# Attention and a mixture of experts on one core: ScalarE issues the weight loads of experts 1 to 7, each two eighths of a product after the split that frees its place

## The chip, the cores and the metric

The kernel runs on one core of a Trainium2 chip. The metric is the time of one execution in microseconds (us) of device time; the median of several runs stands for a kernel. A core has five engines that each take their instructions in order: TensorE (PE, matrix products; its weight loads are shown as PEld), VectorE (DVE), ScalarE (ACT), GpSimd (POOL) and SyncE (SP), which here only issues transfers. Sixteen DMA engines move the data. SP and ACT each feed a DMA queue of their own (q1 and q10 in the profile); POOL feeds a third (q0) with gathers and scatters.

## What is computed

Attention over 8 batches of 8 heads, 576 positions and 64 values a head, with scores below the row's maximum minus tau masked away, and then a mixture of experts on the 4608 rows of 512 values that it gives: each row goes to the one expert with the largest gate logit.

```python
scores = scale * np.matmul(q, k.transpose(0, 1, 3, 2))
thresh = np.max(scores, axis=-1, keepdims=True) - tau
scores = np.where(scores >= thresh, scores, -1000000000.0)
attn = exp(scores - max);  attn = attn / (sum + 1e-09)
x = matmul(attn, v), laid out as (4608, 512)
logits = x @ w_gate;  expert_idx = np.argmax(logits, axis=1)
for e in range(8):
    xe = x[expert_idx == e]
    out[expert_idx == e] = gate_w * (np.maximum(xe @ w1[e], 0.0) @ w2[e])
```

## The kernel before

**The order of the work.** The program is written as a walk over steps `k`. A step computes one tile of scores twice (L294 to L306 for the maxima, L342 to L368 for the transposed scores, the exponential and the mask) and one piece of the product with the values (L400 to L409). Everything else is put into lists by step (`plan`, `after`, `chain`) or by eighths of a product (`moe(c, ready, f)`: run `f` at the c-th eighth, or later when `ready()` holds). An eighth is 12 products of 128 columns on TensorE; the counter is `chunk[0]`. After the program is written, a scheduler moves instructions inside each engine's list by a simulated time of its own, so the built order isn't the written one.

**Rows to experts.** When a batch is finished, `finish(b)` makes the rows `x`: POOL or DVE normalise (L454), ACT casts the high part (L461), DVE or POOL the low part (L462), SP issues one DMA transpose per 128 rows into `xTg` (L469), and TensorE computes the logits (L483). `route` and `ranks` then run on DVE: the logits are reduced (L489), the winner is marked (L509 to L516), `run` counts (L520), TensorE ranks the rows (L528 to L531, `rk`), and DVE makes the place of each row, `posi` (L534 to L541), and ACT the gate (L524, L542). POOL scatters each tile of 128 rows to a DRAM array `xs` sorted by expert (L549). Batch 7, the last, has five tiles.

**The experts.** Each expert has four slots of 128 rows (slots 0 to 31; slots 0 to 7 go one by one, the others in pairs), and four late slots of 192 rows take what is left over. `fetch(m)` gathers the rows of a slot (L744, POOL), transposes them (L747, SP) and copies the gate (L750, DVE) and the destination (L755, POOL). The two tiles named `spare` hold slots 3 and 4. `gemm1` (L792) and `gemm2` (L819) are the two products; ACT takes the ReLU (L780) and the result (L830), POOL scatters it to the output (L831). The first fetches of a batch-7 row need the scatters before them, so on POOL scatters to `xs` and gathers of slots 5, 6 and 7 alternate.

**The weights.** An expert's weights come in eight pieces of 128x1024 f32 (512 KB), named `wf_e_c_w` (expert e, piece c of 4, w = 0 for the first product's matrix and 1 for the second's). `load_w` issues the load; `split_w` makes two f16 parts of it, the high part on ACT (L710), then the low part on DVE (L711). Expert 0 has two places for its pieces, all others share eight. `wseq` lists the pieces in the order of their splits. The first eight of experts 1 and up are loaded by `close`, when the attention's buffers are given back; from then on the split of piece j is followed at once by the load of piece j + 8, on SP, whose list also holds the transposes of L469 and L747.

Of the kernel before, what the change touches and what calls it, by code (L numbers as in the profile page):

```python
# [50 lines left out]
def kernel(  # L51
# [9 lines left out]
    nc = tc.nc  # L61
# [630 lines left out]
    def load_w(e, w, c):  # L692

        i = int(e != 0)
        wq[e, w, c] = wf = pools[i].tile([P, F], F32, tag="wf", name=f"wf_{e}_{c}_{w}", bufs=2 + 6 * i)
        if e in range(E):
            nc.sync.dma_start(wf, w12[e, :, c, w])
            return
        if e not in regs:
            regs[e] = nc.sync.value_load(T["esi"][0:1, e - E:e - E + 1], min_val=0, max_val=E - 1)  # L700
        nc.sync.dma_start(wf, w12[ds(regs[e], 1), :, c, w].rearrange("o p f -> (o p) f"))
# [3 lines left out]
    def split_w(e, w, c):  # L705
        wf = wq.pop((e, w, c))

        o = (wb1, wb2)[w][0 if e == "x" else e % 2][:, c].rearrange("p (a h d) -> p a h d", a=w + 1, h=2)
        x = wf.rearrange("p (a d) -> p a d", a=w + 1)
        nc.scalar.activation(o[:, :, 0], x, AF.Copy, scale=SW)  # L710
        nc.vector.scalar_tensor_tensor(o[:, :, 1], x, SW, o[:, :, 0], ALU.mult, ALU.subtract)  # L711
# [229 lines left out]
    def room():  # L941
        ldp.close()
        open_pool(0)
        load_w(*wseq[0])
        load_w(*wseq[1])

    def close():
        apool.close()
        open_pool(1)
        for i, x in enumerate(wseq[8:16]):  # L950
            after(W1D * i, lambda x=x: load_w(*x))

    wseq = [(0, w, c) for w in range(2) for c in range(4)]
# [11 lines left out]
    chunk = [0]  # L965
    wait = []

    def moe(c, ready, f):
        mo.setdefault(c, []).append((ready, f))
# [49 lines left out]
    def weights(j):  # L1019
        turn[0] = j + 1  # L1020
        split_done.add(wseq[j])
        split_w(*wseq[j])
        if j + 8 < len(wseq):
            load_w(*wseq[j + 8])

    for j, (k, *x) in enumerate(when):
        moe(k, lambda x=x: may(*x), lambda j=j: weights(j + 8))
# [123 lines left out]
```

## Time and profile before

| | us |
|---|---|
| median of 3 runs | 1066.05 (1059.29 to 1070.53) |
| the profiled execution | 1071.58 |
| its span, which the trace covers | 1069.9 |

The trace is of one execution on the only core, some 1.7 us shorter than the device's time of that execution. TensorE is the busiest engine. The span falls into the attention (up to some 600 us), a passage in which the last batches are routed while the first experts begin (some 600 to 740 us), the experts at full speed (740 to 992 us) and the late slots (992 us to the end).

### The profile page before, as it was taken

To read this page: it belongs to the slowest core of one execution; us is meant where nothing else is said; L and a number is where in the kernel's file an instruction comes from. 1 tells how busy PE (TensorE), PEld (TensorE's weight loads), DVE (VectorE), ACT (ScalarE), POOL (GpSimd) and SP (SyncE) were. 2 spreads that over 40 slices of the span, in tenths; PEclk is the share of its full clock that TensorE was granted. 3 is DMA by queue.
4 is the path that set the end of the run, shared out by engine and by line. 5 is a ranking of instruction groups with operands and counts; after the bars stand their busy time and mean duration, and the time that the engine had idled before them with its cause. 6 is when DMAs were issued, how large, how long until landed. Compare 5 with 4: busy or idle time off the path is not lost.

```text
span 1069.9 us, 27336 instructions
## 1 busy us (share of the span) xinstructions
PE 955.9 (89%) x10856; PEld 618.6 (58%) x10856; DVE 722.1 (67%) x1443; ACT 650.7 (61%) x1066; POOL 558.6 (52%) x460
## 2 busy tenths in 40 slices
PE   3799999898999999998995697877999999999995
PEld 1355555465565565564653484656677667667683
DVE  6899989788888889997889854732533423424650
ACT  2588887886888878988776653512433433424641
POOL 3266876976887958969768654143122121222121
PEclk9999999999999999999997799898999999999998
DMA  6534454664565635745535449759746656556720
GB/s 185 142 86 122 128 131 106 153 122 111 132 155 142 154 79 156 155 126 135 125 97 149 90 133 244 221 188 242 220 119 199 184 145 216 148 158 212 224 89 24
DMA packets 142558, 159.10 MB, mean 149 GB/s; under 512 B 96345, under 2 KB 112731, under 8 KB 142428
## 3 DMA queue, kind: packets, MB, share of 16 engines
q1 hardware_dynamic: 126796, 100.35, 38.2%
q10 hardware_dynamic: 6480, 27.53, 8.7%
q0 software_dynamic: 9152, 29.45, 8.6%
q8 instruction: 86, 1.41, 0.6%
q14 instruction: 44, 0.36, 0.1%
HBM read 90.24 MB, written 19.44 MB: 103 GB/s over the span
## 4 chain that ended last, share of the span: by engine, by line
PE 50%; DMA 17%; DVE 11%; issue 9%; ACT 6%; POOL 5%; SPq 2%; POOLq 0%; DVEq 0%; ACTq 0%
PE h L792 14%; PE y L819 12%; PE s L294 4%; PE st L342 4%; DVE e L362 3%; PE st L343 3%; PE s L296 3%; ACT e L359 3%; PE av L408 3%; PE av L409 3%; DMA CQ<-ptT 3%; DVE nm L306 3%; PE av L407 2%; DMA out_dram<-o,gt 2%; DMA xs<-R,posi 2%
## 5 line engine op out<-in xcount | busy, mean ns | idle before, releaser
L368 POOL TENSOR_TENSOR pl<-e,ph 128x1024 f16<-128x1024 f32 x158 | 337.1, 2145 | 135.0 <-ACT ph L367 105.5
L359 ACT ACTIVATE e<-st,ntau 128x512 f32<-128x512 f32 (+1 forms) x352 | 221.8, 651 | 45.6 <-PE st L343 39.4
L362 DVE SCALAR_TENSOR_TENSOR e<-st,e 128x512 f32<-128x512 f32 (+1 forms) x352 | 220.6, 638 | 29.9 <-ACT e L359 29.0
L306 DVE TENSOR_REDUCE nm<-s 128x1 f32<-128x512 f32 x320 | 200.3, 633 | 30.4 <-PE s L296 29.0
L792 PEld LDWEIGHTS <-wb 128*128 128x128 f16 x2304 | 193.2, 100 | 33.2 <-DMA xTm<-R 12.0
L792 PE MATMUL h<-xTm,wb 128*128 128x256 f16 (+2 forms) x2112 | 198.7, 256 | 12.9 <-DMA xTm<-R 12.5
L819 PE MATMUL y<-wb,hl 128*128 128x512 f16 (+1 forms) x1056 | 201.3, 360 | 0.3 <-issue 0.3
L367 ACT CAST ph<-e 128x1024 f16<-128x1024 f32 x160 | 166.4, 1041 | 11.2 <-DVE e L362 11.0
L408 PE MATMUL av<-vop,pl 128*128 128x65 f16 (+1 forms) x1280 | 161.1, 196 | 2.3 <-POOL pl L368 2.2
L294 PE MATMUL s<-QK 128*128 128x512 f16 (+3 forms) x640 | 139.2, 294 | 26.7 <-DMA QK<-lo 17.9
L407 PE MATMUL av<-vop,ph 128*128 128x64 f16 (+1 forms) x1280 | 162.6, 195 | 0.0
L409 PE MATMUL av<-vop,ph 128*128 128x65 f16 (+1 forms) x1280 | 161.8, 196 | 0.0
L342 PE MATMUL st<-QK 128*128 128x512 f16 (+3 forms) x640 | 139.1, 293 | 24.8 <-DVE e L362 15.8
L711 DVE SCALAR_TENSOR_TENSOR wb<-wf,wb 128x1024 f16<-128x1024 f32 x96 | 120.0, 1283 | 53.5 <-ACT wb L710 51.6
L819 PEld LDWEIGHTS <-hl 128*128 128x128 f16 (+1 forms) x1056 | 94.3, 100 | 98.9 <-issue 2.4
L343 PE MATMUL st<-CQ,ck 128*128 128x512 f16 (+3 forms) x640 | 137.7, 291 | 10.4 <-DMA CQ<-ptT 10.4
L408 PEld LDWEIGHTS <-pl 128*128 128x128 f16 (+1 forms) x1280 | 121.9, 101 | 28.3 <-POOL pl L368 9.0
L296 PE MATMUL s<-ck,CQ 128*128 128x512 f16 (+3 forms) x640 | 137.2, 290 | 0.0
L409 PEld LDWEIGHTS <-ph 128*128 128x128 f16 (+1 forms) x1280 | 121.8, 101 | 22.6 <-issue 10.6
L407 PEld LDWEIGHTS <-ph 128*128 128x128 f16 (+1 forms) x1280 | 122.4, 101 | 15.9 <-issue 6.5
L710 ACT ACTIVATE wb<-wf 128x1024 f16<-128x1024 f32 x96 | 97.5, 1050 | 41.9 <-DMA wf<-in_w_dram 21.8
L780 ACT ACTIVATE hl<-h 128x512 f16<-128x512 f32 (+1 forms) x80 | 45.6, 572 | 125.8 <-PE h L792 111.6
(189 smaller groups left out, 1147.0 us busy)
## 6 DMA issues: line engine op xcount, KB each, us to landing
wf<-in_w_dram SPq DMA_DIRECT2D x96, 512.0 KB
qkf<-in_qk_dram ACTq DMA_DIRECT2D x30, 576.0 KB
vf<-in_v_dram ACTq DMA_DIRECT2D x15, 640.0 KB
QK<-hi SPq DMA_DIRECT2D x64, 144.0 KB
QK<-hi SPq DMA_DIRECT2D x64, 72.0 KB
QK<-lo SPq DMA_DIRECT2D x64, 72.0 KB
ck<-lo SPq DMA_DIRECT2D x64, 72.0 KB
CQ<-hi SPq DMA_DIRECT2D x64, 64.0 KB
```

The source lines that it names most:

```text
L294: nc.tensor.matmul(sc[rows, oc], d["QA"][a][:, cols], d["KB"][a][:, CH[c]], start=True, stop=False)
L306: nc.vector.tensor_reduce(o, sc[:, 0:width(t)], axis=AX.X, op=ALU.max, negate=True)
L342: nc.tensor.matmul(sc[rows, oc], d["KB"][a][:, cols], d["QA"][a][:, CH[c]], start=True, stop=False)
L343: nc.tensor.matmul(sc[rows, oc], d["CK"][a][:, cols], d["CQ"][:, q], start=False, stop=True)
L359: nc.scalar.activation(pf, sc, AF.Exp, bias=ntau, scale=0.125 / SS)
L362: nc.vector.scalar_tensor_tensor(pf, sc, 0.0, pf, ALU.is_ge, ALU.mult)
L368: (nc.vector if (n, t) in PLV else nc.gpsimd).tensor_tensor(l, pd, h, ALU.subtract)
L407: nc.tensor.matmul(av[rows, a, 0:D], h, vop[:, tv, W:W + D], start=False, stop=False)
L408: nc.tensor.matmul(av[rows, a], l, vop[:, tv, 0:W], start=False, stop=False)
L409: nc.tensor.matmul(av[rows, a], h, vop[:, tv, 0:W], start=False, stop=a == 1 and i >= 2 and j == NT - 1)
L792: nc.tensor.matmul(o, Wt[:, c, wh, f], x, start=c == 0 and z == 0, stop=c == 3 and z == 2,)
L819: nc.tensor.matmul(o, h[:, hh], Wt[:, f, wh, c], start=f == 0 and z == 0, stop=f == 7 and z == 2)
```

## The change

The loads of experts 1 to 7 are issued by ACT in place of SP; those of expert 0 and of the late slots (whose expert is read from a register on SP) stay on SP. And each load after the first eight is put two eighths of a product behind the split, for the late slots too, while before it followed the split at once.

```diff
@@ load_w
         if e in range(E):
-            nc.sync.dma_start(wf, w12[e, :, c, w])
+
+            (nc.scalar if e else nc.sync).dma_start(wf, w12[e, :, c, w])
             return
@@ weights
         split_w(*wseq[j])
         if j + 8 < len(wseq):
-            load_w(*wseq[j + 8])
+
+            moe(chunk[0] + 2, lambda: True, lambda: load_w(*wseq[j + 8]))
```

The blank lines shift the lines of the changed kernel: L697 of before is L698, L710 is L711, L711 is L712, L747 is L748, L780 is L781. In the rows below, a name is tile, then its numbers (`wf_1_2_1` is expert 1, piece 2, second matrix), then the built program's own number. The scheduler also moves instructions that the change doesn't name.

SP in the passage, before: from the last of the first eight loads to the transposes of slots 3 and 4.

```order
L697 DMA wf_2_0_1_12851<-in_w12_dram 128x1024
L697 DMA wf_2_2_0_12885<-in_w12_dram 128x1024
L469 DMA_TRANSPOSE xTg_7_0_12717<-R_197 128x8x128 x2
L697 DMA wf_1_0_1_12890<-in_w12_dram 128x1024
L697 DMA wf_2_1_1_12950<-in_w12_dram 128x1024
L469 DMA_TRANSPOSE xTg_7_2_12736<-R_197 128x8x128 x2
L697 DMA wf_1_1_1_12966<-in_w12_dram 128x1024
L697 DMA wf_2_3_0_12971<-in_w12_dram 128x1024
L469 DMA_TRANSPOSE xTg_7_4_12747<-R_197 128x8x128
L697 DMA wf_1_2_1_13057<-in_w12_dram 128x1024
L747 DMA_TRANSPOSE spare_12675<-spare_12675 128x8x128 x2
```

The same place now:

```order
L469 DMA_TRANSPOSE xTg_7_0_12717<-R_197 128x8x128 x2
L469 DMA_TRANSPOSE xTg_7_2_12736<-R_197 128x8x128 x2
L469 DMA_TRANSPOSE xTg_7_4_12747<-R_197 128x8x128
L748 DMA_TRANSPOSE spare_12675<-spare_12675 128x8x128 x2
L748 DMA_TRANSPOSE xTm_5_13130<-R_197 128x8x128
```

The loads have left SP's list, and the transposes follow one another.

ACT in the passage, before: the casts of batch 7 (L461) and the splits of expert 1's first matrix.

```order
L710 ACTIVATE wb1_1_12629<-wf_1_0_0_12659 128x1024
L710 ACTIVATE wb1_1_12629<-wf_1_1_0_12724 128x1024
L461 CAST R_197<-xn_7_2_12713 128x4x128
L710 ACTIVATE wb1_1_12629<-wf_1_2_0_12755 128x1024
L461 CAST R_197<-xn_7_3_12722 128x4x128
L830 ACTIVATE o_0_0_12761<-y_0_0_12702,gt_0_0_11605 128x512
L461 CAST R_197<-xn_7_4_12732 128x4x128
L710 ACTIVATE wb1_1_12629<-wf_1_3_0_12835 128x1024
```

The same place now:

```order
L711 ACTIVATE wb1_1_12629<-wf_1_0_0_12659 128x1024
L698 DMA wf_2_0_1_12875<-in_w12_dram 128x1024
L698 DMA wf_1_0_1_12888<-in_w12_dram 128x1024
L711 ACTIVATE wb1_1_12629<-wf_1_1_0_12724 128x1024
L711 ACTIVATE wb1_1_12629<-wf_1_2_0_12755 128x1024
L461 CAST R_197<-xn_7_2_12713 128x4x128
L461 CAST R_197<-xn_7_3_12722 128x4x128
L698 DMA wf_2_2_0_12934<-in_w12_dram 128x1024
L698 DMA wf_2_1_1_12960<-in_w12_dram 128x1024
L711 ACTIVATE wb1_1_12629<-wf_1_3_0_12833 128x1024
L698 DMA wf_1_1_1_12966<-in_w12_dram 128x1024
L461 CAST R_197<-xn_7_4_12732 128x4x128
```

The loads stand between splits and casts; the first of all, `wf_1_0_0`, stands right behind L420, the last copy out of the attention's product. Further on, the load `wf_1_2_1` stands behind the split of `wf_1_0_1`, and `wf_1_3_1` behind that of `wf_1_2_1`.

DVE where batch 7 is routed, before:

```order
L516 TENSOR_REDUCE lg_7_12895<-oh_7_12942 128x8
L711 SCALAR_TENSOR_TENSOR wb2_1_12630<-wf_1_2_1_13057,wb2_1_12630 128x2x512
L520 TENSOR_TENSOR run_151<-run_151,lg_7_12895 128x8
L534 TENSOR_TENSOR rk_7_13019<-rk_7_13019,base_e_116 128x40
L536 TENSOR_REDUCE rk_7_13019<-ex_7_12943 128x5
L537 TENSOR_TENSOR rk_7_13019<-rk_7_13019,oh_7_12942 128x40
L538 TENSOR_SCALAR sm_7_12944<-rk_7_13019 128x5
L539 TENSOR_REDUCE rk_7_13019<-rk_7_13019 128x5
L540 RECIPROCAL sm_7_12944<-sm_7_12944 128x5
L711 SCALAR_TENSOR_TENSOR wb2_1_12630<-wf_1_3_1_13127,wb2_1_12630 128x2x512
L541 CAST posi_7_12946<-rk_7_13019 128x5
```

The same place now:

```order
L516 TENSOR_REDUCE lg_7_12893<-oh_7_12942 128x8
L520 TENSOR_TENSOR run_151<-run_151,lg_7_12893 128x8
L712 SCALAR_TENSOR_TENSOR wb2_1_12630<-wf_1_2_1_13057,wb2_1_12630 128x2x512
L534 TENSOR_TENSOR rk_7_13019<-rk_7_13019,base_e_116 128x40
L536 TENSOR_REDUCE rk_7_13019<-ex_7_12943 128x5
L537 TENSOR_TENSOR rk_7_13019<-rk_7_13019,oh_7_12942 128x40
L538 TENSOR_SCALAR sm_7_12944<-rk_7_13019 128x5
L539 TENSOR_REDUCE rk_7_13019<-rk_7_13019 128x5
L540 RECIPROCAL sm_7_12944<-sm_7_12944 128x5
L541 CAST posi_7_12946<-rk_7_13019 128x5
L712 SCALAR_TENSOR_TENSOR wb2_1_12630<-wf_1_3_1_13127,wb2_1_12630 128x2x512
```

The split of `wf_1_2_1` has moved behind `run`, that of `wf_1_3_1` behind `posi`. A little further on, DVE's copy `gt_5` (L750), which waits for a gather, now stands ahead of the splits of expert 2 and of the low parts of slot 3's and 4's ReLU, where before it stood behind most of them.

TensorE at the ranks of batch 7, before, where they stand behind the first 36 products of slot 3:

```order
L792 MATMUL h_3_0_12980<-spare_12675,wb1_0_11086 128x128
L528 LDWEIGHTS before_103
L528 MATMUL rk_7_13019<-oh_7_12942,before_103 128x8
L531 LDWEIGHTS ones_101
L531 MATMUL rk_7_13019<-was_7_12945,ones_101 128x8
```

The same place now, where they follow the logits:

```order
L483 MATMUL lg_7_12893<-wg_137,xTg_7_4_12747 128x16
L528 LDWEIGHTS before_103
L528 MATMUL rk_7_13019<-oh_7_12942,before_103 128x8
L531 LDWEIGHTS ones_101
L531 MATMUL rk_7_13019<-was_7_12945,ones_101 128x8
```

All of slot 3's first product now stands behind the ranks. Eight products of slot 6's `gemm2` that stood ahead of slot 7's `gemm1` now stand behind it.

## Rows read from the trace of the kernel before

**Rows 1.** The page's first line.

```profile
span 1069.9 us, 27336 instructions
```

**Rows 2.** Windows: length; PE, PEld, DVE, ACT, POOL busy; clock; DMA share; GB/s.

```profile
635.00:662.00 27.00, 26.69 (x289) 17.65 (x286) 16.50 (x32) 12.66 (x22) 11.49 (x8) 1.00 1.03 256
662.00:673.00 11.00, 1.02 (x25) 0.87 (x26) 3.11 (x11) 2.70 (x4) 1.67 (x3) 0.62 1.11 253
...
740.00:992.00 252.00, 252.00 (x1792) 173.83 (x1791) 93.98 (x124) 95.03 (x125) 53.42 (x71) 1.00 0.61 182
```

**Rows 3.** Waits of TensorE, 635 to 745 us: total, times, longest.

```profile
PE h L792 <- DMA xTm<-R: 12.5, 3, 7.8
PE lg L483 <- DMA xTg<-R: 8.4, 2, 5.1
```

**Rows 4.** Timeline of SP: start, duration, what it issued.

```profile
635.52 4.98 SPq L697 DMA_DIRECT2D wf<-in_w_dram  x8
...
651.57 6.24 SPq L469 DMA_TRANSPOSE xTg<-R  x2
657.90 1.01 SPq L697 DMA_DIRECT2D wf<-in_w_dram  x2
659.00 5.90 SPq L469 DMA_TRANSPOSE xTg<-R  x1
665.00 1.49 SPq L697 DMA_DIRECT2D wf<-in_w_dram  x1
```

**Rows 5.** Timeline of ACT; in brackets the idle time before and its releaser.

```profile
638.58 0.26 ACT L420 COPY xh<-av 64x130 f32<-64x130 f32 x1
...
655.02 1.06 ACT L710 ACTIVATE wb<-wf 128x1024 f16<-128x1024 f32 x1 [2.53 <-DMA wf<-in_w_dram]
...
668.00 1.06 ACT L710 ACTIVATE wb<-wf 128x1024 f16<-128x1024 f32 x1 [11.11 <-DMA wf<-in_w_dram]
...
671.93 1.06 ACT L710 ACTIVATE wb<-wf 128x1024 f16<-128x1024 f32 x1 [2.30 <-DMA wf<-in_w_dram]
...
678.34 1.06 ACT L710 ACTIVATE wb<-wf 128x1024 f16<-128x1024 f32 x1 [5.22 <-DMA wf<-in_w_dram]
```

**Rows 6.** Timeline of DVE where batch 7 is routed.

```profile
669.09 1.23 DVE L711 SCALAR_TENSOR_TENSOR wb<-wf,wb 128x1024 f16<-128x1024 f32 x1 [6.48 <-ACT wb L710]
...
671.09 0.25 DVE L489 TENSOR_REDUCE lg<-lg 128x40 f32<-128x80 f32 x1 [0.71 <-PE lg L483]
...
674.16 0.15 DVE L520 TENSOR_TENSOR run<-run,lg 128x8 f16<-128x8 f16 x1
677.50 0.21 DVE L534 TENSOR_TENSOR rk<-rk,base_e 128x40 f32<-128x40 f32 x1 [3.17 <-PE rk L531]
...
678.60 0.18 DVE L540 RECIPROCAL sm<-sm 128x5 f32<-128x5 f32 x1
679.43 1.23 DVE L711 SCALAR_TENSOR_TENSOR wb<-wf,wb 128x1024 f16<-128x1024 f32 x1 [0.65 <-ACT wb L710]
680.57 0.16 DVE L541 CAST posi<-rk 128x5 int32<-128x5 f32 x1
```

**Rows 7.** Timeline of TensorE.

```profile
672.95 4.00 PE L792 MATMUL h<-spare,wb 128*128 128x128 f16 x36 [1.90 <-DMA spare<-spare]
676.74 0.21 PE L528 MATMUL rk<-oh,before 128*128 128x8 f16 x1
...
727.49 7.93 PE L792 MATMUL h<-xTm,wb 128*128 128x128 f16 x92 [7.81 <-DMA xTm<-R]
...
736.53 3.61 PE L819 MATMUL y<-wb,hl 128*128 128x512 f16 x16 [0.34 <-issue]
```

**Rows 8.** Timeline of POOL: the first scatter of batch 7.

```profile
681.51 0.97 POOL L549 DMA_INDIRECT xs<-R,posi  x1 [10.30 <-DVE hl L781]
```

**Rows 9.** ACT's issues of L193 (loads of q and k): ns min/median/max.

```profile
L193 ACTq DMA_DIRECT2D qkf<-in_qk_dram x30: 334/335/412, 12.2 to 509.7; - x30
```

**Rows 10.** Waits in SP's list, whole span, longest total of weight loads.

```profile
SPq L697 <- DVE wb L711: 47.5, 27, 9.3
```

## The prediction

> **What bounds the kernel now.** I read the stages first, then the waits of TensorE, then each engine's timeline in the stretch where TensorE waits. The execution took 1071.58 us, 1.7 us more than its span [rows 1], and lies 5.5 us above the median of the three runs; the sum is made against the execution, and its difference is then applied to the median, 1066.05 us.
>
> From 740 to 992 us TensorE is busy for all of 252 us at the full clock [rows 2]. Most of the moved loads lie there, and nothing there can be gained. What can change is the passage before it. From 662 to 673 us TensorE works 1.02 of 11 us while the DMA share is 1.11: it waits for batch 7's transposes, and the DMA engines are full; they were already from 635 us on (1.03) [rows 2]. Later it waits 12.5 us in three pieces for the transposes of slots 5, 6 and 7, the longest 7.8 us [rows 3], which ends when slot 7 starts at 727.49 us [rows 7]. Slot 7's rows hang on the chain of scatters and gathers on POOL that begins at 681.51 us [rows 8]. POOL's row names a ReLU as its releaser; that is merely the last thing that DVE did. What the scatter needs is `posi`, done just before at 680.57 us [rows 6].
>
> So the question is when `posi` comes. In DVE's list the reduction of the logits (671.09 us) stands behind the low split of `wf_1_1_1` (669.09 us), and `posi` behind that of `wf_1_3_1` (679.43 us) [rows 6]. These splits follow ACT's at 668.00 and 678.34 us, which had waited 11.11 and 5.22 us for their loads [rows 5]. Of the loads, SP issued the first eight at 635.52 us, but the eleventh, `wf_1_1_1`, only at 657.90 and the thirteenth, `wf_1_2_1`, at 665.00 us, behind transposes whose issues took 6.24 us for two and 5.90 us for one [rows 4]. Loads and transposes hold each other up in one list.
>
> **The change, part by part.** *Later start.* The first load now stands behind ACT's copy at 638.58 us [rows 5] in place of 635.52 us [rows 4]: 3.1 us later. If the DMA engines stay full and serve the same bytes, every piece lands 3.1 us later.
>
> *Loads out of SP's list.* The loads no longer wait for transposes to be issued. The eighth in the new order is `wf_1_0_1`, which was the ninth. Thirteen loads took 36.4 us (635.52 to the split at 671.93), 2.8 us each, so one place earlier nearly pays for the later start: its split is at about 655.3 us in place of 655.02 [rows 5]. Right behind it ACT issues the thirteenth load, ten us earlier than SP did. From issue to split the eleventh took 10.1 us (657.90 to 668.00) and the thirteenth 6.9 us (665.00 to 671.93) [rows 4, 5]. With the longer one it would be split at 665.4 us. That is the early end. The late end is work that is merely shifted: 671.93 + 3.1 = 675.0 us. Neither is nearer by a row, since the transposes will now compete with the loads and no row shows them on two queues; I take the middle, 670.2 us, and keep both ends. The eleventh is split 3.9 us before the thirteenth, as before: 666.3 us.
>
> The Trainium skill, page "DMA: Bandwidth & Descriptors", section "Queues, rings and completion order", says that each DMA engine goes round among the queues that have work, a packet at a time; by that the transposes would pass the loads that wait ahead of them now, which is the direction of my middle value, not of the late end.
>
> *The routing of batch 7.* With ACT's part (1.06 us) and DVE's (1.23 us) the eleventh piece is through at 668.6 us, and the reduction starts there, 2.5 us earlier than at 671.09. From it to the end of `run` it is 3.2 us (671.09 to 674.31) [rows 6]: 671.8 us. The ranks then waited until 676.74 us behind 36 products that had begun cold at 672.95 [rows 7]. Now they stand ahead of them: another 2.4 us. From the ranks to DVE's first step it is 0.8 us, from that to the end of the reciprocal 1.28 us (677.50 to 678.78), where `posi` no longer waits for the split of `wf_1_3_1`, which saves 1.8 us. DVE's split of the thirteenth piece now stands ahead of these steps; it ends at 670.2 + 2.3 = 672.5 us, just when the ranks are there (672.6). So `posi` starts at 673.9 and the scatter, 0.94 us behind it as before, at 674.8 in place of 681.51 us: 6.7 us earlier. With the early end it is 670.0 us (11.5 us earlier), with the late end 679.6 us (1.9 us).
>
> *From the scatter on.* I let the 46.0 us from there to slot 7's start [rows 7, 8] stand: the same scatters and gathers alternate, each waiting for the one before it. On DVE the copy `gt_5` moves ahead of the splits of expert 2 and the low parts of slots 3 and 4, so these now wait for a gather. TensorE has 12.5 us of waits in slots 5 to 7 [rows 3] to take that up; if these are used up, every further us counts.
>
> *Eight products of slot 6* filled part of the last wait and now run behind slot 7's first matrix. Sixteen such took 3.61 us [rows 7]: 1.8 us lost.
>
> *Issuing on ACT.* 56 issues at 0.335 us [rows 9] are 18.8 us of ACT's list. From 740 to 992 us ACT is busy for 95 of 252 us [rows 2], so its idle time hides them there; in the passage it is busy 12.66 of 27 and 2.70 of 11 us. I cost them at nothing, with up to 5 us (sixteen issues) if ACT became what TensorE waits for. Each load must also wait until DVE has finished the split that frees its place, and for an earlier transfer on the same completion counter; two eighths later, that is mostly past. The casts, ReLUs and results behind it are what a late one holds up.
>
> *The late slots* keep SP and only get their loads two eighths later: 24 products of 128 columns, at 0.226 us for one of 512 columns [rows 7] some 1.4 us. A load is issued eight pieces ahead of its own split, which covers that; if it didn't, 1.4 us.
>
> Sum: -6.7 + 1.8 = -4.9 us, 1066.7 us for the execution and 1061 us against the median; with the ends, 1056 to 1066.
>
> **The rivals.** *More.* The loads' latency falls to the 6.9 us of the thirteenth before: it is then split at 662.2 us, and only the logits decide, which cannot come before TensorE has finished slot 2 at about 662. Reduction at 662.5, scatter at 668.7: -12.8 + 1.8 = -11.0, 1055 us. For it speaks that fewer loads are outstanding at a time, as each waits for a split; against it the full DMA engines.
>
> *Nothing.* The sixteen DMA engines are the limit (share 1.03 and 1.11 [rows 2]), and who issues doesn't matter: the late end, -1.9 + 1.8, 1066 us. The Trainium skill says this in the same page, section "Issuing engines are not separate DMA queues": issuing from several engines saves only the time of the issue. Against it speak the 6.24 and 5.90 us for which transposes stood in SP's list [rows 4], and that 4.2 us of my gain (ranks and `posi`) come from the order alone.
>
> *Slower: ACT stands still.* What SP could wait out, ACT now waits out in front of casts and ReLUs. SP waited for DVE's splits at these loads 47.5 us in 27 pieces [rows 10], 1.76 us each. Eight such loads (the ninth to the sixteenth) stand ahead of the first scatter and of slot 3's ReLU; at that price they cost 14.1 us: -6.7 + 14.1 + 1.8 = +9.2, 1075 us, and with waits nearer to the longest, 9.3 us, 1080. It decides from 4.9 us of waits on that path, and passes one per cent from 15.6. For it speaks that `wf_1_2_1` and `wf_1_3_1` are now issued only behind another piece's split; against it that SP came to its loads early and ACT comes late.
>
> **How the numbers follow.** One per cent, 10.7 us, is about what a measurement of this kernel can tell from no change. The forecast has a chance of 0.50, more 0.15, nothing 0.21, slower 0.14. Faster by over 1%: 0.10 of the second and 0.07 of the forecast's early tail, 0.17. Slower by over 1%: 0.09 of the last and 0.04 of other tails, 0.13. The rest, 0.70, is within. The range reaches from a little below the early end to the first price of the slow rival: 1053 to 1074.
>
> **What would show it.** Right: SP's transposes of batch 7 with short issues and no load between them; ACT's split of `wf_1_2_1` near 670 us; the ranks ahead of slot 3; the first scatter near 675 us and slot 7's start near 721; a full stretch of 252 us behind it. Wrong: splits near 675 us or later, ACT idle in front of a load with a cast behind it, TensorE waiting for ReLUs of slots 3 to 6, or any idle time of TensorE between 740 and 990 us.

## The result, and the profile after

The changed kernel took 1076.89 us (median of 4 runs, 1069.57 to 1081.42), the kernel before 1062.67 us beside it: a ratio of 1.0119, 95% interval 1.0072 to 1.0166. It is slower by 1.2%; 1061 us was forecast, at most 1074. The profiled execution took 1081.42 us, with a span 9.5 us longer than before [rows 1]:

```profile
span 1079.4 us, 27312 instructions
```

Where the 9.5 us came from is read from the same views. First the windows of the changed kernel, with the columns of [rows 2] (the full stretch now begins at 750 us):

```profile
635.00:662.00 27.00, 22.44 (x276) 16.11 (x273) 16.53 (x32) 12.12 (x21) 9.48 (x8) 0.96 0.89 249
662.00:673.00 11.00, 0.38 (x8) 0.29 (x8) 0.00 (x0) 0.00 (x0) 0.36 (x2) 0.50 1.11 116
750.00:1002.00 252.00, 252.00 (x1791) 173.82 (x1790) 95.65 (x127) 93.52 (x123) 55.15 (x73) 1.00 0.66 184
```

The full stretch is as full as before, now with the loads issued by ACT. The loss is in the passage. From 662 to 673 us hardly any engine works, the DMA engines are as busy as before (1.11), and yet they move 116 GB/s in place of 253. Busy, and moving half: this is the row to follow. The waits of TensorE, 635 to 745 us, say for what:

```profile
PE lg L483 <- DMA xTg<-R: 16.6, 2, 8.6
PE h L793 <- DMA xTm<-R: 8.4, 2, 6.4
```

Against [rows 3] the wait for slots 5 to 7 has shrunk from 12.5 to 8.4 us, as intended, but that for batch 7's transposes has grown from 8.4 to 16.6. SP's timeline, which held transposes of 6.24 us (two) and 5.90 us (one) between loads [rows 4], has now nothing but transposes and is slower at them:

```profile
644.21 31.00 SPq L469 DMA_TRANSPOSE xTg<-R  x5
675.30 4.53 SPq L748 DMA_TRANSPOSE spare<-spare  x2
```

31.00 us for issuing five. And ACT, against [rows 5]: the first load, the twelfth, the split of `wf_1_0_1`, then the thirteenth load, `wf_1_2_1`, and in the last row its split:

```profile
639.46 0.33 ACTq L698 DMA_DIRECT2D wf<-in_w_dram  x1
...
656.11 0.33 ACTq L698 DMA_DIRECT2D wf<-in_w_dram  x1
656.49 0.60 ACT L781 ACTIVATE hl<-h 128x512 f16<-128x512 f32 x1 [2.15 <-DMA wf<-in_w_dram]
656.99 1.05 ACT L711 ACTIVATE wb<-wf 128x1024 f16<-128x1024 f32 x1
674.46 0.38 ACTq L698 DMA_DIRECT2D wf<-in_w_dram  x1
674.93 0.69 ACT L831 ACTIVATE o<-y,gt 128x512 f32<-128x512 f32 x1 [16.90 <-PE lg L483]
675.52 1.05 ACT L711 ACTIVATE wb<-wf 128x1024 f16<-128x1024 f32 x1
...
684.32 1.04 ACT L711 ACTIVATE wb<-wf 128x1024 f16<-128x1024 f32 x1
```

ACT stood 16.9 us in front of that load. The releaser named (PE) is not it: in the built program the load waits for a completion counter that batch 7's second transpose had used, and it was issued the moment this landed (its last part at 674.4 us). DVE's timeline where batch 7 is routed, against [rows 6]:

```profile
683.19 0.25 DVE L489 TENSOR_REDUCE lg<-lg 128x40 f32<-128x80 f32 x1 [5.24 <-PE lg L483]
685.16 0.16 DVE L520 TENSOR_TENSOR run<-run,lg 128x8 f16<-128x8 f16 x1
...
687.69 0.17 DVE L541 CAST posi<-rk 128x5 int32<-128x5 f32 x1
```

TensorE's, from slot 1's second product (`y`) through the logits (`lg`), and slot 7 as in [rows 7]:

```profile
651.88 5.56 PE L820 MATMUL y<-wb,hl 128*128 128x512 f16 x25
666.02 0.38 PE L483 MATMUL lg<-wg,xTg 128*128 128x16 f16 x8 [8.58 <-DMA xTg<-R]
674.43 0.39 PE L483 MATMUL lg<-wg,xTg 128*128 128x16 f16 x8 [8.02 <-DMA xTg<-R]
674.66 7.90 PE L820 MATMUL y<-wb,hl 128*128 128x512 f16 x23
682.40 0.75 PE L483 MATMUL lg<-wg,xTg 128*128 128x16 f16 x24
...
737.41 7.58 PE L793 MATMUL h<-xTm,wb 128*128 128x128 f16 x96 [6.36 <-DMA xTm<-R]
```

And POOL's first scatter of batch 7, against [rows 8]:

```profile
688.64 0.96 POOL L549 DMA_INDIRECT xs<-R,posi  x1 [11.72 <-ACT R L542]
```

The logits are complete 12.1 us later (683.19 against 671.09). From there to the first scatter it is 5.0 us less (5.45 against 10.42), from the scatter to slot 7's start 2.8 more (48.77 against 45.98), from there to the first product of 256 columns 0.1 more (12.60 against 12.49), and behind it 0.5 less: 12.1 - 5.0 + 2.8 + 0.1 - 0.5 = 9.5 us. Of the 12.1 us, 8.0 are the transposes: the last packet of the fifth tile moved at 678.1 us, before at 670.1; up to 1.2 of these 8.0 may be the attention's, which ended later in this execution (639.2 against 638.0). The other 4.1 are TensorE's list: 23 products of slot 2 stood behind the logits that waited, ran only from 674.66 us, and the last logits stood behind them.

Runs more than 1.5% above a kernel's fastest are left out of the ratios; in e3 below one run of 1052.20 us put 4 of 12 out, so that its 0.9953 reads too low (the medians of all runs are 1064.62 and 1064.85 us), and the profiled executions of f2 and g1 are of that kind too.

### The profile page after: what moved, and what is told of

It reads as the page before. It is cut to its first block, busy times and chain, and to the rows that moved or that the text cites. A ratio compares the mean times of both kernels' runs of the same rounds, so it can differ in the third digit from the quotient of the medians.

```text
span 1079.4 us, 27312 instructions
## 1 busy us (share of the span) xinstructions
PE 960.7 (89%) x10856; PEld 619.7 (57%) x10856; DVE 720.6 (67%) x1443; ACT 650.2 (60%) x1066; POOL 559.4 (52%) x460
## 4 chain that ended last, share of the span: by engine, by line
PE 41%; DMA 8%; DVE 4%; ACT 1%; issue 1%; POOL 1%; POOLq 0%; SPq 0%; ACTq 0%; DVEq 0%
PE y L820 17%; PE h L793 17%; DMA xTg<-R 3%; DMA xs<-R,posi 1%; PE st L342 1%; PE st L343 1%; PE s L294 1%; DVE e L362 1%; DVE wb L712 1%; PE av L409 1%; PE av L407 1%; PE av L408 1%; PE s L296 1%; DMA vf<-in_v_dram 1%; DMA R<-xs,row 1%
## 5 line engine op out<-in xcount | busy, mean ns | idle before, releaser
L820 PE MATMUL y<-wb,hl 128*128 128x512 f16 (+1 forms) x1056 | 206.4, 365 | 1.5 <-DVE hl L782 1.5
L712 DVE SCALAR_TENSOR_TENSOR wb<-wf,wb 128x1024 f16<-128x1024 f32 x96 | 118.4, 1268 | 61.4 <-ACT wb L711 61.1
L711 ACT ACTIVATE wb<-wf 128x1024 f16<-128x1024 f32 x96 | 97.5, 1049 | 33.4 <-PE h L793 13.9
L751 DVE COPY gt<-R 128x1 f32<-128x1 f32 x35 | 5.4, 154 | 161.6 <-DMA out_dram<-o,gt 125.9
```

Source lines behind the costliest of these rows:

```text
L820: nc.tensor.matmul(o, h[:, hh], Wt[:, f, wh, c], start=f == 0 and z == 0, stop=f == 7 and z == 2)
```

## The experiments

Theory A, formed on this profile: while the loads move on ACT's queue, each packet of 256 bytes of a transpose (1024 of them for 128 rows) waits for a packet of 4 KB of a load. Rival B: ACT's stand is the cost. Rival C: the two eighths bring the loads too late. Rival D: it is POOL's gathers for slots 3 and 4 that slow the transposes. Each edit is against the changed kernel if nothing else is said.

**e1: ACT, without the two eighths.**

```diff
-            moe(chunk[0] + 2, lambda: True, lambda: load_w(*wseq[j + 8]))
+            load_w(*wseq[j + 8])
```

> ScalarE issues the loads of experts 1 to 7, but each at once behind its split, without the two eighths. Theory A (two queues: while loads of 4 KB packets run on ScalarE's queue, the transposes of batch 7 on SyncE's queue, whose packets have 256 bytes, get only one packet for each of theirs, so the routing comes late): the loads still lie beside the transposes, the logits of batch 7 end at about 683 us as in the changed kernel (671 before), and the time is 8 to 12 us above the kernel before, ratio 1.008 to 1.012. Rival B (ScalarE stands still 16.5 us in front of the load of wf_1_2_1): the load still stands behind another piece's split, so the same sum, and ScalarE again idle 10 us or more there. Rival C (the two eighths bring the loads too late): without them the loss is gone, within 2 us of the kernel before.

Measured: 1.0123 (1.0083 to 1.0163). The loss is all there without the two eighths, so C falls.

**e2: SP, with the two eighths.**

```diff
-            (nc.scalar if e else nc.sync).dma_start(wf, w12[e, :, c, w])
+            nc.sync.dma_start(wf, w12[e, :, c, w])
```

> SyncE issues all loads, as before, but each two eighths after its split. The ranks stand ahead of slot 3 and posi ahead of the split of wf_1_3_1, as in the changed kernel. Theory A: loads and transposes are in one queue again, one behind the other; the transposes of batch 7 end near 671 us as before, the order saves 2 to 5 us from the logits to the first scatter, and the time is 0 to 5 us below the kernel before, ratio 0.995 to 1.000. Rival B gives the same as A. Rival C: the loss stays, 8 to 12 us above the kernel before.

Measured: 1.0001 (0.9967 to 1.0036). The loss is gone; A and B both had this. The order did what was forecast, 6.1 us from the reduction to the scatter in place of 10.4, and the time did not fall by anything that the runs can tell.

**e3 and e4: the change for experts 3 to 7 alone, and for 1 and 2 alone.**

```diff
 e3
+            (nc.scalar if e > 2 else nc.sync).dma_start(wf, w12[e, :, c, w])
+            if wseq[j + 8][0] > 2: moe(chunk[0] + 2, ...)  else: load_w(...)
 e4
+            (nc.scalar if e in (1, 2) else nc.sync).dma_start(wf, w12[e, :, c, w])
+            if wseq[j + 8][0] < 3: moe(chunk[0] + 2, ...)  else: load_w(...)
```

> Only experts 3 to 7 are changed (ScalarE issues, two eighths later; the late slots two eighths later too); experts 1 and 2 as before. All of A, B and C put the loss into the passage at 640 to 690 us, where only experts 1 and 2 load: within 3 us of the kernel before, TensorE full from 740 to 990 us. If issuing on ScalarE costs something in the full stretch, or loads of expert 3 beside the transposes of slots 5 to 7 do, 3 to 8 us above.

> Only experts 1 and 2 are changed (ScalarE issues, two eighths later); experts 3 to 7 and the late slots as before. By A, B and C the whole loss is here: 8 to 12 us above the kernel before, ratio 1.008 to 1.012, logits of batch 7 complete near 683 us. If instead the loss were spread over all loads, under 4 us.

Measured: e3 no difference (0.9953, read as said above), e4 1.0105 (1.0069 to 1.0141). The sixteen loads of experts 1 and 2 carry the loss; the 40 of experts 3 to 7 show no cost on ACT.

**f1: the same loads in packets of 1 KB.**

```diff
-... = pools[i].tile([P, F], F32, tag="wf", ...)
+... = pools[i].tile([P, F + 4 * i], F32, tag="wf", ...)
+            if e in (1, 2):
+                nc.scalar.dma_start(
+                    wf.rearrange("p (b f) -> p b f", b=4)[:, :, 0:F // 4],
+                    w12[e, :, c, w].rearrange("p (b f) -> p b f", b=4),
+                )
```

> As the changed kernel, but the loads of experts 1 and 2 are written into rows with a gap of one element after each 256, so that they move in packets of 1 KB in place of 4 KB; the bytes are the same. Theory A (each 256-byte packet of a transpose waits for one packet of the load on the other queue, 0.16 us for 4 KB): with packets a quarter as long the transposes of batch 7 go two to three times as fast beside the loads; their last packet comes at 668 to 674 us in place of 679, and the time falls 4 to 10 us below the changed kernel, to a ratio of 1.001 to 1.007. Rival D (it is the gathers of slots 3 and 4 on GpSimd's queue, not the loads, that slow the transposes): no difference, ratio 1.009 to 1.014. Rival B (ScalarE's stand in front of wf_1_2_1 is the cost, whatever makes it): the stand ends when the second transpose lands, so it goes with A.

Measured: 1.0024 (0.9993 to 1.0055). By this ratio four fifths of the loss is gone, with the same bytes, the same issuer and the same order; the rest is too small to be told from nothing (g4 below). SP's timeline of f1 shows it,

```profile
650.19 20.75 SPq L469 DMA_TRANSPOSE xTg<-R  x5
```

and so does the window that stood still in the changed kernel:

```profile
662.00:673.00 11.00, 8.13 (x43) 3.29 (x41) 2.61 (x3) 3.84 (x7) 5.11 (x7) 0.84 1.12 351
```

Issuing the five takes 20.75 us in place of 31.00, and from their first packet to their last it is 22.0 us (654.1 to 676.1) in place of 29.9 (648.2 to 678.1). In the window that stood still TensorE works 8.13 us and 351 GB/s move; attention had ended 5.3 us later here, which makes a part of that. The packets themselves, counted from the DMA records of the traces (number and mean time):

```
kernel, us of its span    load packets            transpose packets, 256 B
before  671.3 to 673.3    none                    2048 x 18 ns   (1024 per us)
after   648 to 654        4 KB:  538 x 167 ns      530 x 18 ns   (  88 per us)
f1      660 to 675        1 KB: 3268 x  48 ns     3384 x 19 ns   ( 226 per us)
g3      675 to 684        512 B: 3159 x 30 ns     3144 x 19 ns   ( 349 per us)
after   658 to 673        4 KB:  181 x 197 ns     1604 x 91 ns   ( 107 per us)
after   674 to 676        4 KB:    7              1890 x 20 ns   ( 945 per us)
```

The second, third and fourth line are A in its plainest form: one for one, so that the transposes' rate follows from the length of the other queue's packet (sixteen engines over 167 + 18 ns are 86 per us, over 48 + 19 ns 239, over 30 + 19 ns 327). The times of the single records say the same: from 649 to 654 us, with chance taken off, some 470 of the 489 transpose packets end just where a load packet starts.

**f2: ACT does not stand.**

```diff
+            if (e, w, c) == (1, 1, 2):
+                pad = tp.tile([1, 4], F16, name="pad")
+                for i in range(2):
+                    nc.sync.dma_start(pad[:, 2 * i:2 * i + 2], wb2[1][0:1, 0, 2 * i:2 * i + 2])
```

> As the changed kernel, with two 4-byte copies added on SyncE behind the last transpose of batch 7. They shift the rotation of the eight completion counters, so that the load of wf_1_2_1 on ScalarE waits for the completion of wf_2_2_0 and no longer for that of batch 7's second transpose. ScalarE should issue it near 658 us and go on. Theory A (the transposes are slow because loads move beside them): the transposes stay as slow or become slower, since one more load runs beside them, and the time is within 3 us of the changed kernel, ratio 1.008 to 1.015. Rival B (ScalarE's stand of 16.5 us is the cost): the loss goes, ratio 0.998 to 1.004.

Measured: 1.0135 (1.0080 to 1.0191). ACT's timeline of f2 has the load of `wf_1_2_1` at 665.35 us, with 1.7 us of idle time around it:

```profile
665.35 0.35 ACTq L702 DMA_DIRECT2D wf<-in_w_dram  x1
665.80 0.69 ACT L835 ACTIVATE o<-y,gt 128x512 f32<-128x512 f32 x1 [1.74 <-DVE wb L716]
```

SP's timeline of f2 has the transposes of batch 7, slower still:

```profile
650.57 37.98 SPq L469 DMA_TRANSPOSE xTg<-R  x5
```

ACT stands again behind the next load, 19.3 us, but for a product of TensorE, behind logits that wait for these transposes. B falls: the stand was a consequence. It seems even to have spared the transposes a load; without it 37.98 us go into issuing the five.

**f4: the gathers held until the transposes are done.**

```diff
+            if m in (NF, NF + 1):
+                nc.gpsimd.tensor_copy(Rm[:, 0:1], got7[B - 1, 4][:, 0, 0:2].bitcast(I32))
             nc.gpsimd.indirect_dma_start(Rm, None, xs[:, :], ...)
```

> As the changed kernel, but GpSimd's two gathers for slots 3 and 4 wait until the last transpose of batch 7 has landed (a copy of one element from it stands ahead of each). Theory A (loads beside transposes): the transposes of batch 7 stay slow while the first twelve loads move, so their last packet comes at 668 us or later; slot 3 starts some 8 us behind it, and the time is within 4 us of the changed kernel, ratio 1.007 to 1.015. Rival D (gathers beside transposes): the transposes end by 664 us, the logits come 12 us or more earlier than in the changed kernel, and the time is at or below the kernel before, ratio 0.994 to 1.003.

Measured: 1.0107 (1.0073 to 1.0140), with the last packet of the fifth tile at 679.6 us and no gather moving before 682.6. D falls for the changed kernel. POOL's scatters of results still moved, 64 packets of 4 KB between 664 and 671 us.

**g3: packets of 512 bytes.** The edit is f1's with eight pieces for four.

> As f1_thin, with a gap after each 128 elements, so that the loads of experts 1 and 2 move in packets of 512 bytes. Theory A (packet for packet between the two queues): the 1 KB packets of f1 took 0.048 us each and stood one for one with the transposes' packets (0.018 us); at 512 bytes a packet takes some 0.025 to 0.03 us (an estimate, half of that and a fixed part), so a pair takes 0.045 in place of 0.066 us: the five tiles of batch 7 pass in 15 to 17 us beside the loads (22 us in f1, from 654.2 to 676.2), and the time is 2 to 5 us below f1, ratio 0.998 to 1.001. The loads themselves get slower by as much, which can cost: if ScalarE then waits for the pieces longer, ratio 1.002 to 1.006. Rival (f1 gained from something else in the layout): as f1 or slower, with the transposes as fast as there.

Measured: 1.0047 (1.0014 to 1.0081). The pairs are as expected (the line of g3 above), the sum is not: the five tiles took 22.6 us (656.0 to 678.6) and not 15 to 17. From 669 to 672 us only 188 transpose and 223 load packets moved, a fifth of the rate behind it. One packet for one holds; it does not tell the whole time, and a shorter packet than 1 KB brought no more.

**What stays open there.** By pairs alone the changed kernel's transposes would be through at about 663 us: some 950 of their 5120 packets meet a load packet (11 us from 648), the rest need 4 to 5 us. That is earlier than in the kernel before (670.1). They took until 678.1, so the loss lies in the stretch from 658 to 673 us, and the pairs don't explain it. Only 181 load packets were left there, 12 per us, and the transposes still went at 107 per us. Right behind the last of these load packets they went at nearly full rate: 94 in the microsecond before it was through, 767 and 1062 in the two after; in e4 62, then 745 and 1120, in f4 68, then 724 and 1055; only in e1 it took 4 us more.

The landing records tell a part of it. A load lands in sixteen parts of eight packets each, read here as one part for each DMA engine. Those of the twelfth load landed from 662.6 to 674.2 us, those of the second transpose all at 673.9 to 674.4; in f1 the parts of the twelfth load landed within 1.6 us (673.1 to 674.7). So in the changed kernel the engines had come far apart, and the transposes were through when the last had caught up. But it isn't a matter of a few engines that still alternate: at 666 us 13 of the 16 parts were missing, and 13 engines with a pair in 0.185 us would move 70 load packets per us, not 12. The packets themselves were slow in this stretch: 91 ns for a transpose's in place of 18, 679 ns for the gathers' of 4112 bytes. Nor is it POOL's queue alone: in f4 it moved nothing from 672 to 675 us, and the transposes had 609 packets in these 3 us. What holds them all until the last load packet is gone, the traces don't tell; the runs show that it comes with loads of experts 1 and 2 on the other queue (e1, e4), that the time isn't lost when SP issues them (e2), and that the length of their packets decides most of it (f1).

**f3, g1, g2: can the order's gain be had without the loss?** All three have SP issue the loads. f3 is e2 with slot 6's second product ahead of slot 7's first; g1 is the kernel before with f4's held gathers; g2 is e2 with them. g4 is the kernel before again.

```diff
 f3
+            for f in fs[::-1] if i in (7,) else fs:   # fs: first product of i, second of i - 1
+                yield from f()
```

> SyncE issues all loads, each two eighths later (the kernel e2_sp_later), and the second product of slot 6 is put ahead of the first product of slot 7. In e2 the order had brought the first scatter of batch 7 some 4 us forward without a gain in the time; TensorE stood 7.3 us before slot 7 with the 24 products of slot 6 (5.2 us) queued behind it. If that is where the gain went, this kernel is 4 to 6 us below e2 and the kernel before: ratio 0.994 to 0.997. If slot 7's rows only come later in turn, the ratio is 0.999 to 1.002.

> The kernel before (SyncE issues, no delay), with the two gathers of slots 3 and 4 held until the last transpose of batch 7 has landed, as in f4_hold. It asks whether gathers slow the transposes where no loads run beside them: in the kernel before the third and fourth tile took from 655.8 to 665.4 us while the gathers moved, the first two 2.4 and 1.2 us. If gathers do that, the fourth tile is through 5 to 8 us earlier against the end of attention, the logits come earlier by that, and the time falls 2 to 6 us, ratio 0.994 to 0.998. If they do not, the gathers only come later and slot 3 with them: ratio 1.002 to 1.008.

> The candidate that takes what held: SyncE issues all loads, each two eighths later (the ranks and posi stand early, as in e2), and the gathers of slots 3 and 4 wait for the last transpose of batch 7 (as in g1). The first scatter should come 32 to 35 us after the end of attention (43.5 and 41.6 us in the two profiles of the kernel before). If the chain from the scatter to slot 7 keeps its 46 us, slot 7 starts 7 us earlier than before and the ratio is 0.990 to 0.994. If TensorE's own work from the logits to slot 7 is what sets slot 7, as g1 hints (scatter 7 to 9 us earlier, slot 7 only 2 to 4), the ratio is 0.994 to 0.999.

> The kernel before once more, unchanged, for a second profile of it: how much of a difference between two single profiles is the run's own. Ratio 0.997 to 1.003; the end of attention and the passage from there to the first product of 256 columns may each differ by several us from the first profile (638.0 and 102.0 us).

Measured: f3 1.0038 (1.0000 to 1.0076), g1 0.9944 (0.9914 to 0.9975), g2 0.9970 (0.9940 to 1.0000), and g4, which is the same program, 0.9962 (0.9932 to 0.9992). The interval of g4 leaves out 1 for one and the same program, and so half a per cent is not told apart here. f3 shows no gain (it lies above both of its ranges), g1 and g2 are no gain that can be claimed, and no version is shown to beat the kernel before. Not run: the loads on ACT's queue, held until the transposes are through. In g1 the transposes did gain from the gathers' absence: the fourth tile was through 1.0 us after the third (5.7 in the kernel before, 4.6 in g4, 2.6 in e2), and SP's timeline shows the last one at 1.25 us (5.90 in [rows 4]),

```profile
667.73 1.25 SPq L472 DMA_TRANSPOSE xTg<-R  x1
```

but what TensorE no longer waits for slots 5 to 7 (12.5 us in [rows 3]) it waits elsewhere, 635 to 760 us of g1:

```profile
PE y L824 <- DVE hl L786: 6.3, 1, 6.3
PE pc L572 <- DVE posi L544: 3.9, 1, 3.9
PE h L797 <- DMA xTm<-R: 3.4, 1, 3.4
```

Times of the profiles side by side, us; the end of the attention is the start of its last product. It fell between 635.7 and 649.1 us, so a single profile is good for some 5 us only. e1's, with the latest end, is 9.0 us behind the kernel before at three quarters of the attention's products already, ahead of any moved load; it shows the passage from there no longer than before (101.6 us against 102.0), and for e1 the ratio is the evidence.

| | end of attention | last packet of batch 7 | first scatter | slot 7 | first 256-wide product | ratio |
|---|---|---|---|---|---|---|
| before | 638.0 | 670.1 | 681.5 | 727.5 | 740.0 | 1 |
| g4 (before again) | 635.7 | 665.8 | 677.3 | 723.0 | 735.4 | 0.9962 |
| e2 | 642.4 | 670.2 | 677.3 | 723.4 | 736.1 | 1.0001 |
| g1 | 647.6 | 673.0 | 681.9 | 733.2 | 745.4 | 0.9944 |
| f1 | 644.5 | 676.1 | 683.3 | 730.0 | 742.2 | 1.0024 |
| after | 639.2 | 678.1 | 688.6 | 737.4 | 750.0 | 1.0119 |
| e1 | 649.1 | 680.3 | 690.5 | 738.8 | 750.7 | 1.0123 |
| e4 | 644.5 | 680.7 | 690.6 | 736.0 | 748.5 | 1.0105 |
| f4 | 643.9 | 679.6 | 689.9 | 734.4 | 747.5 | 1.0107 |
| f2 | 645.3 | 691.0 | 698.0 | 744.4 | 756.5 | 1.0135 |

## Why the prediction was wrong

*The step that failed* is "Loads out of SP's list". It counted what the transposes cost the loads in one list and took that as the gain; what the loads would cost the transposes on two queues was named ("the transposes will now compete with the loads") and got no term. The forecast therefore let the routing hang on the loads (the eleventh piece's split, 668.6 us), and took the transposes as done in time in any case. It took the middle for want of a row, and read the Trainium skill's round of queues as letting the transposes pass, "the direction of my middle value". The Trainium skill, page "DMA: Bandwidth & Descriptors", section "Queues, rings and completion order", says that an engine goes round among its queues a packet at a time; the traces agree, one for one in after, f1 and g3. But a turn for a turn gives 256 bytes for each 4 KB: the transposes pass the loads at 88 packets per us where, behind them in one list, they had waited and then gone at 1024. And behind the pairs came 15 us at 107 per us, in which the transposes lost what they had gained; the cause of this second part stays open. The routing came 14.6 us later than forecast (reduction at 683.19 against 668.6).

*The thirteenth piece.* "Right behind it ACT issues the thirteenth load, ten us earlier than SP did": it was issued at 674.46 us, 9.5 us later than SP did, and split at 684.32, past the late end of 675.0. The wait for an earlier transfer on the same counter was named and called "mostly past"; with slow transposes it was not.

*The order.* Right: ranks and `posi` earlier were worth 5.0 us from the reduction to the scatter (4.3 in e2), 4.2 forecast.

*"I let the 46.0 us stand."* 48.8 in after and 46.1 in e2, but 51.3 in g1 and 49.3 in g2, where the gathers were held: there an earlier scatter was not as much earlier a slot 7. In e2's profile slot 7 starts 81.0 us after the end of the attention in place of 89.5 (87.3 in g4), and its runs still show no gain. For the order alone the prediction's own terms give 4.2 - 1.8 = 2.4 us, and e2's interval reaches to 3.5 us of gain: this part is neither shown nor refuted. The whole forecast of -4.9 us for transposes that are left undisturbed was not put to a run.

*Later start, issues, late slots, eight products.* The loads began 3.9 us later (3.1 forecast). ACT's issues and the late slots show no cost, as said (e3; 329.4 us from the first 256-wide product to the end, 329.9 before). The eight products were priced at 1.8 us and show as 0.1.

*The rivals.* "Slower: ACT stands still" gave 1075 us with a chance of 0.14, near the 1076.89 measured, and ACT did stand, in front of a load with a cast behind it, as the list of signs had it. But it was the right size for another reason: f2 took the stand away and the time stayed. "Nothing" leaned on the same page of the Trainium skill, section "Issuing engines are not separate DMA queues", by which issuing from two engines saves issue time and no more. The runs differ: sixteen loads moved to the other engine's queue, with their two eighths, cost 1.05% (e4), and the move without the two eighths 1.23% (e1). The same bytes in the same time is not the same order of arrival.

## What to carry to other kernels

Before a transfer is moved to a second queue, look at what runs on the first beside it and in what packets: many small packets that somebody waits for do well in front of or between large ones in one list, and badly beside packets of 4 KB on two. A window in which the DMA share is full and the GB/s are half is the sign, and the length of the other queue's packets the handle (f1). A load that is issued by a computing engine also brings its waits into that engine's list, so look up which earlier transfers its wait covers.

## What the runs showed of the hardware

While two queues both had packets waiting, these alternated one for one, at 4 KB, 1 KB and 512 bytes alike; a packet of 4 KB of a load took 0.167 us in the mean, of 1 KB 0.048, of 512 bytes 0.030, and one of 256 bytes of a transpose 0.018. Beside a tail of 12 load packets of 4 KB per us the transposes went at a tenth of their rate (107 per us against 1024), mostly until the last one had gone, while the sixteen parts of one load landed 11.6 us apart (after); why is not shown. With gathers on a third queue the fourth tile needed 2.6 to 5.7 us (e2, g4, before), without them 1.0 (g1), and holding them back returned no time that the runs can tell apart.
